# Batch 0's z on the way in: two direct tiles instead of six, group 1's z over four column tiles, a raw load for the state, and a wide state tile of its own for batch 1

## The chip, the cores and the metric

One NeuronCore of a Trainium2 chip runs the kernel. The figure is device time in microseconds of one launch; the kernel before takes 694.18 us in the median of three runs (694.01 to 696.45). TensorE (PE) multiplies, with its weight loads listed apart (PEld); VectorE (DVE), ScalarE (ACT) and GpSimd (POOL) work elementwise; SyncE (SP) issues most DMAs, ACT a few.

## What is computed

Eight batches of 512 tokens and 32 state rows, eight heads of 64. Tokens read the state, the state reads the tokens, and both results, 8 x 544 = 4352 rows of 512, go through a feed-forward layer with a squared ReLU, all in float32:

```python
scores = scale * np.matmul(x, state.transpose(0, 1, 3, 2))        # per batch and head: 512 x 32
a = softmax(scores);   xread = np.matmul(a, state)                # the tokens' result
scores2 = scale * np.matmul(state, x.transpose(0, 1, 3, 2))       # 32 x 512
a2 = softmax(scores2); sread = np.matmul(a2, x)                   # the state's result
y = np.concatenate([xread, sread], axis=2)                        # then as rows (b, s), heads side by side
r = np.maximum(y @ w_in, 0.0)                                     # 512 -> 2048
out = (r * r) @ w_out                                             # 2048 -> 512
```

## The kernel before

**The products.** For the tokens, `xread @ w_in` is not formed from `xread`. Since `xread = a @ state`, the kernel builds `z = state @ w_in` per batch (head by head, 256 rows of (head, state) by 2048 columns), and a unit of work is one batch and one column tile `fc` of 128 columns: an *up* product `ph` = z' a (L773, six matmuls of 512 columns: high by high, low by high, high by low, for two groups of heads), ReLU on ACT (L779), square on DVE or ACT (L785, L787), the split into a high and a low part `g_hi` (ACT) and `g_lo` (DVE, L345), and a *down* product into four accumulators `po` (L809, twelve matmuls). Most operands are such high and low pairs: ACT casts the high part, DVE or POOL subtracts (the helper `split`, L340 and L345).

**The units** run in the order of `PARTS`: batch 0 with column tiles 0 to 5, batch 1 with all sixteen, batch 0 with 6 to 15, then batches 2 to 7, and in the end the state rows of all batches together. The first visit to batch 0 is there while weights still come in; its partial sums go to DRAM and come back.

**z.** Batches 0 to 3 are group 0, 4 to 7 group 1. For group 0, `z_part` (L429) multiplies the state of four batches by two column tiles of `w_in` in plain float32 (L439), 16 blocks in all, two 64-row halves side by side; ACT copies the result to `z_stage` (L464) and stores it to DRAM (`zd`). For group 1 the same function runs in the middle of the kernel with split operands (L451, twelve matmuls of 256 columns a block). `z_fetch` (L500) reads one batch's rows back in four loads of 64 KB and splits them into `z_hi`, `z_lo`. For the first six column tiles (`DIRECT`) of batch 0, `z_direct` (L479) makes z on the spot from a block-diagonal state tile `sp_f` (L486, tile `pzd`), with no way through DRAM.

**Scores.** `sq` (L563) multiplies x by the same `sp_f` for batches 0 and 1; from it come, over transposes `sT` and `pa`, the softmax weights `a_hi`, `a_lo` that an up product needs, and `e2` for the other softmax. Batch 0's state is loaded straight into `sp_f`, batch 1's later copied over it (L535).

**Weights** arrive as 64-bit words and are turned into float32 in four steps each (`singles`, ACT L356, DVE L360, L365, L371): `wi` tiles from `w_in`, `wof` and then `wo_hi`, `wo_lo` from `w_out`. Their raw tiles share four slots (tag `raw`).

**The order** on each engine comes from a planner. Every operation states an engine and a cost, its operands, a due time or earliest time; the planner runs a list schedule for several settings (`FIRST` by `SLACKS`), takes the one that ends first by its own costs, and issues in that order. All engines then run their queues in order, and wait for each other by semaphores. `keep_busy` (L836) gives PE small filler matmuls for planned gaps.

## Time and profile before

| | |
|---|---|
| median of three runs | 694.18 us |
| the profiled execution itself | 694.38 us |
| its span, first to last instruction | 692.6 us |
| PE busy | 682.9 us, 99% |
| ACT, DVE, POOL busy | 432.7, 376.7, 158.7 us |
| granted PE clock | 1.00 throughout |
| first up product (`ph`) starts | 21.40 us |
| batch 1's first up product | 62.79 us |

The profile numbers time from the first instruction. "Busy" of PE counts from the start of a matmul to its modelled end, so that the starts of neighbouring matmuls, not their durations, tell the pace. A row of the timeline gives start, length, engine, source line, what is written from what, how many instructions, and in brackets the idle time before and what ended it.

### The profile page before, as it was taken

The page shows a single profiled execution, that of the slowest core. Times are in us where ns is not written, and L with a number is a line of the kernel's source. Part 1 is how long each engine was busy: PE and PEld are TensorE (multiplying, and loading weights), DVE is VectorE, ACT ScalarE, POOL GpSimd, SP SyncE. Part 2 cuts the span into 40 slices and gives each one's busy share as a digit, 9 for nine tenths or more (in the row PEclk, how much of TensorE's full clock was granted, in tenths as well). Part 3 has the DMA queues.
Part 4 walks back from the last instruction along what each step waited for, and adds up shares of the span by engine and source line. Part 5 has one row for each costly group of instructions (what it writes and reads, how often), then busy time and mean ns, then how long its engine had stood idle before and what let it go on. Part 6 is the DMA issues. An engine that isn't in the chain of part 4 may idle for free.

```text
span 692.6 us, 9920 instructions
## 1 busy us (share of the span) xinstructions
PE 682.9 (99%) x3416; PEld 549.0 (79%) x3416; DVE 376.7 (54%) x657; ACT 432.7 (62%) x819; POOL 158.7 (23%) x174
## 2 busy tenths in 40 slices
PE   8999999999999999999999999999999999999997
PEld 7767777778888887777887888888888888888886
DVE  5999889284386556423342574673853433223431
ACT  4788778686565766666565675775655555443552
POOL 0010003243333354111222353363423210000000
PEclk9999999999999999999999999999999999999999
DMA  8778884352122313533233222222232112100101
GB/s 290 256 268 283 300 289 149 126 185 89 54 91 87 96 46 127 177 141 122 80 117 127 92 78 98 88 91 62 91 102 82 31 31 91 32 1 0 62 1 32
DMA packets 50371, 79.05 MB, mean 114 GB/s; under 512 B 6928, under 2 KB 32656, under 8 KB 50320
## 3 DMA queue, kind: packets, MB, share of 16 engines
q1 hardware_dynamic: 45248, 60.84, 27.4%
q10 hardware_dynamic: 5072, 17.57, 6.4%
q8 instruction: 27, 0.44, 0.3%
q14 instruction: 24, 0.20, 0.1%
HBM read 51.64 MB, written 26.74 MB: 113 GB/s over the span
## 4 chain that ended last, share of the span: by engine, by line
PE 95%; DMA 2%; ACT 1%; DVE 1%; issue 0%; ACTq 0%
PE po L809 55%; PE ph L773 28%; PE pr L714 2%; PE pz L439 2%; PE pz L451 2%; PE pq L584 2%; DMA w_raw<-w_in 1%; PE idle L836 1%; PE pt L696 1%; DMA out<-os__2977 1%; PE sq L563 1%; PE pzd L486 1%; DVE wi L365 0%; ACT z_stage L464 0%; ACT r L779 0%
## 5 line engine op out<-in xcount | busy, mean ns | idle before, releaser
L809 PE MATMUL po<-wo_hi,g_hi 128*128 128x512 f32 x544 | 218.8, 402 | 2.2 <-ACT g_hi L340 1.1
L809 PE MATMUL po<-wo_lo,g_hi 128*128 128x512 f32 x544 | 214.4, 394 | 0.0
L345 DVE TENSOR_TENSOR g_lo<-ph,g_hi 128x512 fp32r<-128x512 f32 (+1 forms) x144 | 94.5, 657 | 138.9 <-PE po L809 108.5
L809 PE MATMUL po<-wo_hi,g_lo 128*128 128x512 f32 x544 | 155.7, 397 | 0.0
L340 ACT CAST g_hi<-ph 128x512 fp32r<-128x512 f32 (+1 forms) x144 | 81.1, 563 | 95.2 <-PE po L809 92.1
L779 ACT ACTIVATE r<-ph 128x512 f32<-128x512 f32 (+1 forms) x144 | 82.7, 574 | 88.9 <-PE ph L773 88.6
L809 PEld LDWEIGHTS po<-wo_hi,g_hi 128*128 128x128 f32 x544 | 102.4, 188 | 28.0 <-ACT g_hi L340 2.0
L809 PEld LDWEIGHTS po<-wo_lo,g_hi 128*128 128x128 f32 x544 | 102.5, 188 | 20.6 <-DVE wo_lo L345 0.2
L809 PEld LDWEIGHTS po<-wo_hi,g_lo 128*128 128x128 f32 x544 | 99.6, 188 | 23.8 <-issue 1.8
L787 DVE TENSOR_TENSOR ph<-ph,r 128x512 f32<-128x512 f32 (+1 forms) x66 | 45.0, 682 | 131.8 <-ACT r L779 131.5
L345 POOL TENSOR_TENSOR xn_hl<-xn_raw,xn_hl 128x512 fp32r<-128x512 f32 x32 | 45.5, 1423 | 193.9 <-ACT xn_hl L340 193.9
L773 PE MATMUL ph<-a_lo,z_hi 128*128 128x512 f32 x256 | 80.9, 396 | 0.0
L773 PE MATMUL ph<-a_hi,z_lo 128*128 128x512 f32 x256 | 80.7, 396 | 0.0
L773 PE MATMUL ph<-a_hi,z_hi 128*128 128x512 f32 x256 | 80.2, 394 | 0.1
L773 PEld LDWEIGHTS ph<-a_lo,z_hi 128*128 128x128 f32 x256 | 48.2, 188 | 11.8
L773 PEld LDWEIGHTS ph<-a_hi,z_lo 128*128 128x128 f32 x256 | 48.1, 188 | 11.1
L773 PEld LDWEIGHTS ph<-a_hi,z_hi 128*128 128x128 f32 x256 | 47.9, 188 | 11.2 <-PE idle L836 0.2
L345 POOL TENSOR_TENSOR xt_hl<-xt_raw,xt_hl 128x512 fp32r<-128x512 f32 x24 | 32.9, 1370 | 81.0 <-ACT xt_hl L340 81.0
L345 DVE TENSOR_TENSOR z_lo<-z_raw,z_hi 128x512 fp32r<-128x512 f32 x61 | 45.3, 742 | 3.0 <-ACT z_hi L340 3.0
L785 ACT ACTIVATE ph<-r 128x512 f32<-128x512 f32 (+1 forms) x78 | 44.4, 569 | 1.9
L464 ACT COPY z_stage<-pz 128x512 f32<-128x512 f32 x64 | 34.5, 592 | 12.1 <-PE pz L451 8.7
L340 ACT CAST z_hi<-z_raw 128x512 fp32r<-128x512 f32 x61 | 37.5, 616 | 2.6 <-DMA z_raw<-zd 2.3
(135 smaller groups left out, 752.6 us busy)
## 6 DMA issues: line engine op xcount, KB each, us to landing
zd<-z_stage ACTq DMA_DIRECT2D x32, 512.0 KB, 3.0
z_raw<-zd SPq DMA_DIRECT2D x244, 64.0 KB, 2.4
w_raw<-w_in SPq DMA_DIRECT2D x16, 512.0 KB, 5.7
wo_raw<-w_out SPq DMA_DIRECT2D x16, 512.0 KB, 5.5
xn_raw<-xn SPq DMA_DIRECT2D x16, 512.0 KB, 4.2
xt_raw<-xT SPq DMA_DIRECT2D x15, 512.0 KB, 3.8
part<-part SPq DMA_DIRECT2D x4, 256.0 KB, 3.5
xt_raw<-xT ACTq DMA_DIRECT2D x1, 512.0 KB, 3.4
```

The lines of the kernel that those rows point to most:

```text
L340: act(n, 0.03 if both else 0.0), lambda e: nc.scalar.copy(out=hi(), in_=src()),
L345: lambda e: ENGINE[e].tensor_sub(out=lo(), in0=src(), in1=hi().bitcast(F32)),
L439: nc.tensor.matmul(pz[i].t[:, q, :], lhsT=st[G].t[own, cc, :], rhs=wi[own, k * FPC:(k + 1) * FPC, cc, :], start=True, stop=True,)
L451: nc.tensor.matmul(pz[i].t[:, q, :], lhsT=s_hl.t[own, m, cc, :], rhs=w_hl[w].t[own, :, cc, :], start=j == 0, stop=j == 2,)
L464: act(512), lambda e, i=i: nc.scalar.copy(out=stage.t[:, :, i, :], in_=pz[i].t),
L584: nc.tensor.matmul(pq.t, lhsT=sp_hl[:, g, q].rearrange("p i n -> p (i n)"), rhs=hl.t[:, i], start=i == 0, stop=i == 1,)
L714: nc.tensor.matmul(pr.t[:, q].rearrange("p i c -> p (i c)"), lhsT=eh.t[:, t, q].rearrange("p i n -> p (i n)"), rhs=hl.t[:, t].rearrange("p ...
L773: nc.tensor.matmul(ph.t[:, :width], lhsT=w, rhs=v, start=j == 0, stop=j == len(pairs_) - 1)
L779: act(width), lambda e: nc.scalar.activation(rl.t[:, :width], ph.t[:, :width], AF.Relu),
L785: nc.scalar.activation(ph.t[:, :width], rl.t[:, :width], AF.Square)
L787: nc.vector.tensor_mul(out=ph.t[:, :width], in0=ph.t[:, :width], in1=rl.t[:, :width])
L809: nc.tensor.matmul(po[t].t, lhsT=(g[0], g[0], g[1])[j].t[:, t * P:(t + 1) * P], rhs=wo[k][j % 2][:, i, :], start=first and j == 0, stop=la ...
```

## The change

Six things change together. `DIRECT` is 2 in place of 6, so batch 0's column tiles 2 to 5 take z from the `z_part` blocks through DRAM. Group 1's blocks are made by a new function `z_quad`: one pair of heads over four column tiles, six matmuls of 512 columns, in place of two pairs over two column tiles, twelve of 256. Batch 0's state comes through a raw tile and two DVE copies, as batch 1's did. Batch 1 has a wide tile of its own, cleared by POOL. `sp_f` is no constant any more but shares a slot with `e_hl`, and its clearing on DVE stands behind that of the filler's operand. And the planner has other costs for matmuls, an earlier `START` and four values of `FIRST`.

```diff
 def pe(n, k=1):
-    return ("PE", k * (0.0134 + n / 2400))
+    return ("PE", k * (0.006 + n / 2265))
...
+    FPQ = 2 * FPC
...
-    DIRECT = 6
+    DIRECT = 2
...
-    START, FIRST, STEP = 14.0, (3.5, 4.4), 4.4
+    START, FIRST, STEP = 8.0, (3.0, 3.5, 4.0, 4.4), 4.4
...
-    sp_f = const.tile([P, NG, 2, P + D], F32, name="sp_f")
-    nc.vector.memset(sp_f, 0.0)
+    sp_f = tile_([P, NG, 2, P + D], F32, "sp_f", "e_hl")
+    op(("DVE", 0.7), lambda e: nc.vector.memset(sp_f.t, 0.0), w=[(sp_f, 0), (sp_f, 1)], due=-90.0)
...
+    def z_quad(kq, g, q, w_hl, begin):
+
+        pz = [tile_([P, FPQ * P], F32, f"pz{i}", "px") for i in range(2)]
+        stage = tile_([P, 2, FPQ * P], F32, "zq_stage", "z_stage")
+        s_hl = halves["st"]
+
+        def products(e):
+            for j, (m, w) in enumerate(((0, 0), (1, 0), (0, 1))):
+                for i in range(2):
+                    own = slice(i * D, (i + 1) * D)
+                    nc.tensor.matmul(
+                        pz[i].t, lhsT=s_hl.t[own, m, g * NQ + q, :], rhs=w_hl[w].t[own, :, q, :],
+                        start=j == 0, stop=j == 2,
+                    )
...
+        src = zq[k // 2][at:at + N, :, :, (k % 2) * FW:(k % 2 + 1) * FW] if b >= GB else zd[k][at:at + N]
...
     def pad(b):
...
-        if b == 0:
-            for i in range(2):
-                load(
-                    lambda i=i: sp_f[rows[i], :, :, at[i]], lambda i=i: src[rows[i]], 32,
-                    w=[f"sp_f{i}"], issue=0.6, due=-60.0,
-                )
-            return
         raw = tile_([P, NG, 2, N], F32, "sp_raw")
-        load(lambda: raw.t, lambda: src, 64, w=[raw])
+        load(lambda: raw.t, lambda: src, 64, w=[raw], due=1e9 if b else -60.0)
         for i in range(2):
             if b < PLAIN_X:
+                if i == 0:
+                    wide[b] = tile_([P, NG, 2, P + D], F32, "sp_f1", "x_hl") if b else sp_f
+                    if b:
+                        op(("POOL", 0.9), lambda e: nc.gpsimd.memset(wide[b].t, 0.0), w=[(wide[b], 0), (wide[b], 1)])
...
-        op(("PE", 0.4), product, w=[ph], begin=0.4 * k)
+        op(("PE", 0.4), product, w=[ph], begin=1.2 + 0.4 * k)
...
-                w_halves(k, At(at - 1))
-                for g in range(NG):
-                    z_part(1, k, g, begin=At(at))
+                w_hl = w_halves(*divmod(m, NG), At(at - 1))
+                for q in range(NQ):
+                    z_quad(*divmod(m, NG), q, w_hl, At(at))
```

**SP, the first loads.** `sp_f` and `sp_raw` are batch state, `w_raw` and `wo_raw` weight tiles, `xt_raw` x for the scores, `st_z` the state for `z_part`. Before:

```order
L379 DMA sp_f<-stP 64x4x32 x2
L379 DMA w_raw<-w_in 128x1024
L379 DMA xt_raw<-xT 128x2x512
L379 DMA w_raw<-w_in 128x1024
L379 DMA wo_raw<-w_out 128x1024
L379 DMA w_raw<-w_in 128x1024
L379 DMA st_z<-stT 64x4x128 x2
L379 DMA sp_raw<-stP 128x128
L379 DMA xt_raw<-xT 128x2x512
```

Now:

```order
L378 DMA sp_raw<-stP 128x128
L378 DMA w_raw<-w_in 128x1024 x3
L378 DMA xt_raw<-xT 128x2x512
L378 DMA st_z<-stT 64x4x128 x2
L378 DMA w_raw<-w_in 128x1024
L378 DMA sp_raw<-stP 128x128
L378 DMA xt_raw<-xT 128x2x512
L378 DMA w_raw<-w_in 128x1024
L378 DMA xt_raw<-xT 128x2x512
L378 DMA w_raw<-w_in 128x1024
L378 DMA wo_raw<-w_out 128x1024 x3
```

Three weight tiles of `w_in` now stand ahead of batch 0's second x tile, and all six that the first visit needs ahead of the first of `w_out`.

**DVE, up to batch 0's second `a_lo`.** Before, the stretch in which both groups' `a_lo` are made:

```order
L643 TENSOR_TENSOR q_270<-q_270,s_313 128x512
L643 TENSOR_TENSOR q_299<-q_299,s_324 128x512
L360 TENSOR_SCALAR wof<-wof 128x512
L360 TENSOR_SCALAR wi<-wi 128x512
L365 SCALAR_TENSOR_TENSOR wof<-wo_raw,wof 128x512
L345 TENSOR_TENSOR a_lo<-pa,a_hi 128x512 x2
L365 SCALAR_TENSOR_TENSOR wi<-w_raw,wi 128x512
L360 TENSOR_SCALAR wi<-wi 128x512 x2
```

Now:

```order
L344 TENSOR_TENSOR a_lo<-pa,a_hi 128x512
L644 TENSOR_SCALAR s_372<-s_372 128x16
L645 RECIPROCAL s_372<-s_372 128x16
L359 TENSOR_SCALAR wi<-wi 128x512
L649 TENSOR_TENSOR q_335<-q_335,s_372 128x512
L364 SCALAR_TENSOR_TENSOR wi<-w_raw,wi 128x512
L359 TENSOR_SCALAR wof<-wof 128x512
L370 SCALAR_TENSOR_TENSOR wi<-w_raw,wi 128x512
L364 SCALAR_TENSOR_TENSOR wof<-wo_raw,wof 128x512
L344 TENSOR_TENSOR a_lo<-pa,a_hi 128x512
L370 SCALAR_TENSOR_TENSOR wof<-wo_raw,wof 128x512
```

The two groups, side by side before, are now one after the other, with steps of weight tiles between; the sixth `w_in` tile is finished ahead of the second `a_lo`.

**PE, from the second up product (before) and the first (now).** Before:

```order
L773 MATMUL ph<-a_hi,z_hi 128x512 x2
L773 MATMUL ph<-a_hi,z_lo 128x512 x2
L773 MATMUL ph<-a_lo,z_hi 128x512 x2
L486 MATMUL pzd<-wi,sp_f 128x128 x8
L809 MATMUL po_467<-wo_hi_85,g_hi 128x512
L809 MATMUL po_467<-wo_lo_86,g_hi 128x512
L809 MATMUL po_473<-wo_hi_85,g_hi 128x512
L809 MATMUL po_473<-wo_lo_86,g_hi 128x512
L486 MATMUL pzd<-wi,sp_f 128x128 x4
```

Now:

```order
L779 MATMUL ph<-a_hi,z_hi 128x512 x2
L779 MATMUL ph<-a_hi,z_lo 128x512 x2
L779 MATMUL ph<-a_lo,z_hi 128x512 x2
L471 MATMUL pz_469<-wi,st_z 128x256
L471 MATMUL pz_470<-wi,st_z 128x256
L471 MATMUL pz_469<-wi,st_z 128x256
L471 MATMUL pz_470<-wi,st_z 128x256
L779 MATMUL ph<-a_hi,z_hi 128x512 x2
L779 MATMUL ph<-a_hi,z_lo 128x512 x2
L779 MATMUL ph<-a_lo,z_hi 128x512 x2
L569 MATMUL sq<-xt_raw,sp_f_119 128x512 x2
```

The direct tiles (`pzd`) are gone from between the up and down products; between the first two up products stands a block of `z_part`, behind them one of batch 1's `sq`.

More of the change, by code (lines that the diff above doesn't have):

```diff
@@ L320, in memory_attention_then_relu2_ffn @@
     ]
-    zd = {
-        (G, k): dr.tile([P, NG, HG, FW], F32, name=f"zd_{G}_{k}")
-        for G in range(NGB) for k in range(NFCH)
-    }
+    zd = [dr.tile([P, NG, HG, FW], F32, name=f"zd_{k}") for k in range(NFCH)]
+    zq = [dr.tile([P, NG, HG, FPQ * P], F32, name=f"zq_{k}") for k in range(NFCH // 2)]
     units = [(b, fc) for b, lo, hi in PARTS for fc in range(lo, hi)]
@@ L418, in z_halves, with w_halves @@
         halves["st"] = hl
-    def w_halves(k, begin):
-        hi, lo = (tile_([P, FPC, NCC, P], F32R, n, "raw") for n in ("wz_hi", "wz_lo"))
-        for i in range(FPC):
+    def w_halves(kq, g, begin):
+        hi, lo = (tile_([P, FPQ, NQ, P], F32R, n, "raw") for n in ("wz_hi", "wz_lo"))
+        for i in range(2):
+            own = slice(i * FPC, (i + 1) * FPC)
             split(
-                lambda i=i: hi.t[:, i], lambda i=i: lo.t[:, i], lambda i=i: wi[:, k * FPC + i], NCC * P,
-                [("wi", k * FPC + i)], [(hi, i)], [(lo, i)], engs=[dve(512), gps(512)], chain="w1", begin=begin,
-            )
-        halves[k] = hi, lo
@@ L430, in z_part, with z_store @@
+    def z_store(pz, stage, out, keys, part, order):
+        for i in range(2):
+            op(
+                act(512), lambda e, i=i: nc.scalar.copy(out=part(i), in_=pz[i].t),
+                r=[pz[i]], w=[(stage, i)],
+            )
+        load(
+            out, lambda: stage.t.rearrange(order), 512,
+            r=[(stage, 0), (stage, 1)], w=keys, eng="ACT", issue=0.35, hold=None, land=4.5,
+        )
+    def z_part(k, g):
         pz = [tile_([P, NQ, FW], F32, f"pz{i}", "px") for i in range(2)]
@@ L506, in z_fetch @@
                 lambda j=j: raw.t[j * N:(j + 1) * N], lambda j=j: src[:, :, j, :], 64,
-                r=[("zd", b // GB, k, g) for g in range(NG)], w=[(raw, j)], issue=0.62, hold=30.0, chain="zf",
+                r=[("zd", b // GB, k, g, q) for g in range(NG) for q in range(NQ)], w=[(raw, j)], issue=0.62, hold=30.0, chain="zf",
             )
@@ L513, in z_fetch @@
         )
-    pairs, kept = {}, {}
+    pairs, kept, wide = {}, {}, {}
     def pad(b):
@@ L563, in product @@
                     nc.tensor.matmul(
-                        sq.t, lhsT=sp_f[:, g].rearrange("p q n -> p (q n)")[:, q * P:(q + 1) * P],
+                        sq.t, lhsT=wide[b].t[:, g].rearrange("p q n -> p (q n)")[:, q * P:(q + 1) * P],
                         rhs=xt.t[:, q, :], start=q == 0, stop=q == NQ - 1,
                     )
-            op(("PE", 1.75), product, r=["sp_f0", "sp_f1", xt], w=[sq])
+            op(("PE", 1.77), product, r=[(wide[b], i) for i in range(2)] + [xt], w=[sq])
             pst = tile_([P, S], F32, "st")
@@ L852, in memory_attention_then_relu2_ffn @@
     for m in range(NFC):
-        z_part(0, *divmod(m, NG))
+        z_part(*divmod(m, NG))
     spill = {}
```

57 lines of the change are left out of this document (21 added, 36 removed).

## The prediction

> **What bounds the kernel now.** I read the page's first lines, then the table by stage, then the waits of TensorE (PE), then the timeline of the first 65 us. Columns of the table: stretch, its length, busy us of PE, PEld, DVE, ACT, POOL with instruction counts, granted clock, DMA share, GB/s.
>
> ```profile
> PE 682.9 (99%) x3416; PEld 549.0 (79%) x3416; DVE 376.7 (54%) x657; ACT 432.7 (62%) x819; POOL 158.7 (23%) x174
> ```
> ```profile
> 0.00:21.40 21.40, 18.97 (x169) 15.12 (x169) 12.69 (x27) 10.96 (x20) 1.17 (x7) 1.00 0.83 284
> ...
> 21.40:62.80 41.40, 40.35 (x207) 30.17 (x206) 40.88 (x80) 33.27 (x68) 3.26 (x2) 1.00 0.76 261
> 62.80:160.00 97.20, 96.01 (x457) 73.05 (x457) 75.39 (x131) 75.14 (x142) 20.34 (x22) 1.00 0.62 213
> ```
> ```profile
> PE idle L836 <- DVE warm L313: 1.8, 1, 1.8
> PE pzd L486 <- DVE wi L371: 1.5, 2, 1.0
> PE po L809 <- ACT g_hi L340: 1.1, 1, 1.1
> PE po L809 <- ACT os__3026 L825: 1.0, 1, 1.0
> ```
>
> PE is full at the full clock, and all its named waits are 5.4 us. So from some 25 us on the time falls only if PE has less to do. Before that PE is not the bound: the first 21.4 us hold much filler, and from 21.4 to 62.8 us DVE is as full as PE (40.88 and 40.35 of 41.40), with ACT at 33.27. Two engines in step is what the change has to deal with; from 62.8 to 160 us DVE has 22 us free.
>
> The rows of the start, then the pace of each engine:
>
> ```profile
> 0.74 0.45 ACTq L379 DMA_DIRECT2D xt_raw<-xT  x1
> 1.69 1.32 SPq L379 DMA_DIRECT2D sp_f<-stP  x2
> 3.06 0.60 SPq L379 DMA_DIRECT2D w_raw<-w_in  x1
> 6.83 0.67 ACT L356 ACTIVATE wi<-w_raw 128x512 f32<-128x512 f32 x1 [4.32 <-DMA w_raw<-w_in]
> 7.53 0.43 DVE L360 TENSOR_SCALAR wi<-wi 128x512 int32<-128x512 int32 x1 [5.79 <-ACT wi L356]
> 8.37 0.83 PE L836 MATMUL idle<-warm 128*128 128x128 bf16 x12
> 9.04 1.94 PE L563 MATMUL sq<-xt_raw,sp_f 128*128 128x512 f32 x4
> 15.69 1.13 PE L439 MATMUL pz<-wi,st_z 64*128 64x256 f32 x8
> 19.12 1.57 PE L439 MATMUL pz<-wi,st_z 64*128 64x256 f32 x8
> 19.93 1.07 ACT L340 CAST a_hi<-pa 128x512 fp32r<-128x512 f32 x2 [0.42 <-ACT z_stage L464]
> 20.55 1.29 DVE L345 TENSOR_TENSOR a_lo<-pa,a_hi 128x512 fp32r<-128x512 f32 x2 [0.79 <-ACT a_hi L340]
> 21.40 0.71 PE L773 MATMUL ph<-a_hi,z_hi 128*128 128x512 f32 x2
> 22.36 0.76 DVE L360 TENSOR_SCALAR wi<-wi 128x512 int32<-128x512 int32 x2
> 25.17 1.89 DVE L371 SCALAR_TENSOR_TENSOR wi<-w_raw,wi 128x512 int32<-128x512 int32 x3
> 26.00 2.02 PE L486 MATMUL pzd<-wi,sp_f 128*128 128x128 f32 x16 [0.99 <-DVE wi L371]
> 34.35 0.45 DVE L535 COPY sp_f<-sp_raw 64x128 f32<-64x128 f32 x2
> 59.62 1.07 ACT L340 CAST a_hi<-pa 128x512 fp32r<-128x512 f32 x2 [0.40 <-PE pa L652]
> 60.58 1.28 DVE L345 TENSOR_TENSOR a_lo<-pa,a_hi 128x512 fp32r<-128x512 f32 x2
> 62.79 2.81 PE ph L773 x12
> ```
>
> Two landmarks: the first up product (`ph`) starts at 21.40 us, and the seventh, batch 1's first, at 62.79. DVE, back to back, takes (1.89 - 0.68) / 2 = 0.60 us for an operation on 512 words and 0.76 - 0.42 = 0.34 for L360. PE takes 0.231 us for a 512-column product:
>
> ```profile
> 291.47 2.05 PE po L809 x8
> 296.75 2.05 PE po L809 x8
> 603.00 2.75 PE po L809 x12
> 607.16 2.75 PE po L809 x12
> ```
> A plain unit is 18 products in 607.16 - 603.00 = 4.16 us; a unit with one of group 1's z blocks in it takes 296.75 - 291.47 = 5.28, so such a block costs 1.12.
>
> **The change part by part.** The sum is made against the profiled execution's own 694.38 us (692.6 of span and 1.8 around it); the median, 694.18, is 0.2 less.
>
> *Four direct z tiles fewer.* Two tiles took 2.02 us in 16 records, so (2.02 - 0.28) / 15 = 0.116 a record and 0.93 a tile of 8: PE loses 3.7 us of work. Its z columns come from the z_part blocks that were run anyway. ACT and DVE trade four half-size splits for two whole ones (0.60 against twice 0.33), nothing. Eight fetches of 64 KB are added; below.
>
> *Quads.* PE's block in the middle of the run, before:
>
> ```profile
> 290.49 0.50 PE L451 MATMUL pz<-wz_hi,st_hl 64*128 64x256 f32 x4
> 290.83 0.28 PE L451 MATMUL pz<-wz_lo,st_hl 64*128 64x256 f32 x2
> 290.95 0.40 PE L451 MATMUL pz<-wz_hi,st_hl 64*128 64x256 f32 x4
> ```
> The two 64-row halves of a pair run together, and a pair of 256 columns takes 290.95 - 290.83 = 0.12 us. Six pairs are 0.72; three pairs of 512 columns, at 0.231 each, 0.69. The rest of the 1.12 lies at the block's two edges, and there are 16 blocks and 32 edges as before. Gain 0.03 x 16 = 0.5 us; bounds 0 and, if the 512-column pair runs at exactly twice 0.107, 1.3. I take 0.4. That goes by what the surplus hangs on: 290.83 - 290.49 is 0.34 for two pairs, the other pairs take 0.12, so it lies where the block begins and ends. The Trainium skill, "TensorEngine Tiling (Array Packing)", section Instruction Overhead, gives each matmul some 60 cycles of overhead; 96 matmuls fewer would then save 2.4 us (an estimate from that page at 2.4 GHz), and the sum would be 2 us lower; the row of 0.12 us for a pair of 256 columns, half of 0.231 and 0.004 more, does not agree.
>
> *The start.* SP's first loads waited for DVE's memset of `sp_f` (1.69) and took 0.66 each, so the first weight tile went out at 3.06. Now one load goes to a raw tile, with no wait; ACT's queue shows that 0.74 is possible, so the weight tile goes out near 1.2, and DVE starts on it 1 to 1.9 us sooner: at 6.0, since it shares the queue with three loads more.
>
> But DVE is given more ahead of the first up. Up to the second `a_lo` of batch 0, before: 16 operations of 0.60, 4 of 0.34, one z_lo of 0.33, four small ones together 0.7: 12.0 us, which from 7.53 to 21.84 took 14.3, so 2.3 us of waits. Now: 24 of 0.60, 7 of 0.34, z_lo, the small ones and four copies into the wide tiles (0.45 a pair): 18.8 us, because all six weight tiles are finished ahead of that `a_lo` instead of two and parts of others. From 6.0, with 1.7 us of waiting for the first `st` copy (the first `sq`, 1.94 us, has to run and be copied): 26.5. DVE is the late engine there, not DMA: six weight tiles, three x tiles and the rest are 5 MB, which the 284 GB/s of the first row move in 18 us. So the **first up starts near 26.3 us instead of 21.4**, 4.9 later. Bounds: 24.8 (no wait) and 27.5 (2.3 us as before and 0.6 for the slower start).
>
> PE meanwhile gets work done that stood behind the first up: one `sq` (1.94) and one z_part (1.13 to 1.57, I take 1.3).
>
> *From first to seventh up.* Before 62.79 - 21.40 = 41.4. Now PE has less between: 3.7 (direct), 1.94 and 1.3 (done earlier), nine `po` of the sixth unit behind the seventh up (9 x 0.231 = 2.1), against four transposes `pt` of 128 columns that came forward (4 x 0.116 = 0.5). 41.4 - 8.5 = 32.9: without waits the seventh up would be at 59.2. DVE's work from `a_lo` of batch 0 to that of batch 1 is 31.4 us by the same count (38.8 before, and there it never waited: 21.84 + 38.8 = 60.6, as the row at 60.58 says), so DVE allows 57.9. ACT's operations between the `a_hi` of batch 0 and of batch 1, each at its mean in the groups, add up to 31 us against 34 before, which took 39.7 (19.93 to 59.62), thus some 5.8 of waits. If ACT waits as long again, batch 1's `a_hi` comes at 25.5 + 36.9 = 62.4 and the seventh up at 63. Between 59.2 and 63, I take 60.9: all three engines now hand to each other with 2 us of slack, and an in-order queue turns such slack into small waits. **1.9 us sooner than before.**
>
> The fetches are covered, though not by much. Column pair 1's second z_part is stored near 21 us and landed at 24. Its fetch stands on SP behind a `wo_raw` load whose slot DVE frees right behind the second `a_lo`, at 27; its four loads leave by 30 and take 5.2, the two splits 1.3: 36.5.
>
> ```profile
> zd<-z_stage ACTq DMA_DIRECT2D x32, 512.0 KB, 3.0
> ```
> ```profile
> z_raw<-zd SPq DMA_DIRECT2D x8, 64.0 KB, 5.2
> ```
> ```profile
> SPq L379 <- DVE wof L371: 22.5, 6, 9.1
> ```
> The first row is the whole run's list of DMA issues, the second that of the first 60 us, the third SP's waits in these 60 us (total, times, longest). PE asks for it at 26.3 plus two ups (2.8), two z_parts (2.6), `sq` (1.94) and twenty `po` (4.6): 38.2. Cover of 1.7 us, and each us past it is a us of PE.
>
> *Behind the seventh up.* PE has the nine `po` to make up, less `pt`: +1.6. The 1.1 us wait for `g_hi` stands where two up products run back to back ahead of a down product; in the new order single ups alternate with downs there: -1.1 (bounds 0 and 1.1). The wait for `os__3026` (1.0) lies where a fourth copy waits for one of three buffers to be written out, and that stays: 0. DVE takes over 44 of the squares that ACT did, and batch 1's wide tile its two copies: with 22 us free up to 160, nothing; were DVE full they would cost 0.60 each.
>
> Sum: -1.9 + 1.6 - 1.1 - 0.4 = -1.8, so 692.6 on the profiled scale and **692.4 us** in the median. Of the 3.7 us taken from PE the slower first up eats about half.
>
> **The rivals.**
> (A) *PE stays dense once it has begun.* Then the seventh up is 1.7 us sooner, and 0.8 more if DVE waits little ahead of the first: -2.5 more, 689.9. For it: in the same stretch before, PE lost 1.05 us in all (40.35 of 41.40); against it: DVE was full there too, and its order is now the one that PE follows.
> (B) *The fetch is late: slower.* Up products 3 to 6 now hang on store, fetch and split. SP's longest wait for a `wof` slot in the first 60 us was 9.1 us. If the fetch of pair 1 stands behind such a wait it goes out at 36 instead of 30 and is split at 42.5: ups 3 and 4 stall for 4 us, and pair 2's, next in the same queue, for 2: 698.4. It decides from 38.2 on. Against it: the slot comes free early in DVE's new order.
> (C) *Cold clock.* The filler ahead of the first `sq` shrinks from 48 matmuls to 32. Before, the filler took 4.97 us:
>
> ```profile
> 1.79 4.97 PE L836 MATMUL idle<-warm 128*128 128x128 bf16 x48 [1.79 <-DVE warm L313]
> ```
> that is 0.10 us apiece, against 0.83 / 12 = 0.07 and less later on, so PE sped up at its end. With 32 the first `sq` could run at half pace, 1.9 us longer, and DVE's chain starts as much later: 694.3. The Trainium skill, "TensorE: Matmul & The Clock Gate", Part 1, says the same of the mechanism: about 3.4 us of activity and not a number of matmuls. The trace agrees in kind: the pace changed 4 to 5 us after the first filler.
> (D) *The quads save more.* If a block's surplus over its columns, 1.12 - 6 x 0.115 = 0.43 us, went with the count of its matmuls and not with its edges, half of it would go, 0.21 x 16 = 3.4, 3.0 more than the sum has: 689.4. The 0.34 of the first two pairs is against it.
>
> **How the numbers follow.** Forecast 0.54 (own range 690.8 to 694.4), A 0.25, B 0.13, C 0.06, D 0.02. A change of under 0.5%, 3.5 us, is about what a measurement here cannot tell from none. Faster than 690.7: A, D and a little of the forecast's edge, less what of A falls short, 0.27. Slower than 697.7: most of B, 0.10. Same: 0.63. The range leaves out A's best (first up at 24.8, `os_` wait gone: 688.2) and B's worse half: 688.8 to 696.2.
>
> **What would show it.** First `ph` between 24.8 and 27.5 us; the seventh between 59.2 and 63; `pzd` with 16 records in place of 48; blocks of `pz` in the middle at 1.09 us instead of 1.12; no PE wait for `z_raw` or its split. I am wrong if the first up starts no later than before, if PE's waits between 26 and 60 us exceed 3 us, or if the stretch behind 160 us differs by over 1.5 us.

## The result: 687.91 us, 6.2 less than before, where 692.4 was predicted

The changed kernel takes 687.91 us (686.67 to 688.96), beside it the kernel before 694.1 (693.56 to 696.45): a ratio of 0.9904, interval 0.9874 to 0.9933. The forecast was 692.4 with a range of 688.8 to 696.2, so the time lies below the range, and the gain is over three times the one I worked out. The span of the one profiled execution fell from 692.6 to 685.5 us, 7.1 us, against 1.8 in the sum.

The table by stage of the changed kernel, cut at the same landmarks: start to the first up product (`ph`), to the seventh (batch 1's first), to the 33rd (batch 2's first), to the end. Columns: stretch, length, then PE, PEld, DVE, ACT, POOL busy with counts, granted clock, DMA share, GB/s.

```profile
0.00:25.69 25.69, 22.18 (x189) 16.56 (x189) 19.55 (x43) 14.16 (x26) 1.85 (x8) 1.00 0.94 336
25.69:58.84 33.15, 31.90 (x163) 23.73 (x161) 32.56 (x63) 28.22 (x59) 2.47 (x2) 1.00 0.73 240
58.84:184.69 125.85, 125.66 (x593) 98.27 (x591) 93.10 (x159) 88.14 (x165) 30.92 (x35) 1.00 0.55 186
184.69:685.50 500.81, 496.31 (x2351) 401.94 (x2349) 272.53 (x454) 267.63 (x511) 123.11 (x131) 1.00 0.24 79
```

The same view of the kernel before, for the two later stretches:

```profile
62.63:188.69 126.06, 124.87 (x591) 96.87 (x590) 87.57 (x151) 91.33 (x171) 29.49 (x35) 1.00 0.53 180
188.69:692.60 503.91, 498.89 (x2455) 407.01 (x2453) 235.74 (x403) 297.28 (x562) 124.82 (x131) 1.00 0.24 78
```

The timeline of the changed kernel at the start and at the two landmarks, and of the kernel before at the seventh up (a closer window puts it at 62.63; the prediction's row, over a longer one, at 62.79):

```profile
0.99 3.60 PE L842 MATMUL idle<-warm 128*128 128x128 bf16 x32 [0.99 <-DVE warm L314]
1.19 1.36 SPq L378 DMA_DIRECT2D w_raw<-w_in  x3
5.11 1.95 PE L569 MATMUL sq<-xt_raw,sp_f 128*128 128x512 f32 x4 [0.52 <-DMA xt_raw<-xT]
6.97 0.43 DVE L359 TENSOR_SCALAR wi<-wi 128x512 int32<-128x512 int32 x1 [2.72 <-ACT wi L355]
25.69 0.71 PE L779 MATMUL ph<-a_hi,z_hi 128*128 128x512 f32 x2
58.84 0.63 PE L779 MATMUL ph<-a_hi,z_hi 128*128 128x512 f32 x2
```
```profile
62.63 0.62 PE L773 MATMUL ph<-a_hi,z_hi 128*128 128x512 f32 x2
```

The four largest waits of PE behind its first filler in the changed kernel (total, times, longest; two more are 0.2 us each):

```profile
PE ph L779 <- DVE g_lo L344: 1.2, 1, 1.2
PE sq L569 <- DMA xt_raw<-xT: 1.0, 2, 0.5
PE pz L471 <- DVE wi L370: 0.7, 1, 0.7
PE pzd L495 <- DVE wi L370: 0.4, 1, 0.4
```

Read against the prediction's fences: the first up is 4.29 us later, the seventh 3.79 sooner, the 33rd 4.00 sooner (184.69 for 188.69), and from there to the end another 3.1 us go, where the sum had 0.4. The waits for `g_hi` at 143 us and for `os__3026` at 277 us are both gone.

The second half can be timed with two rows per kernel, since the order of PE's work hardly differs there: the start of the 65th up (batch 4's first) and of the 121st.

```profile
344.24 0.39 PE L773 MATMUL ph<-a_hi,z_hi 128*128 128x512 f32 x1
601.44 0.39 PE L773 MATMUL ph<-a_hi,z_hi 128*128 128x512 f32 x1
```
```profile
338.48 0.40 PE L779 MATMUL ph<-a_hi,z_hi 128*128 128x512 f32 x1
594.52 0.40 PE L779 MATMUL ph<-a_hi,z_hi 128*128 128x512 f32 x1
```

The first fence is of the kernel before, the second of the changed one: 257.20 and 256.04 us. There is no wait in it and nothing that the change edits but four of the quads' blocks (0.1 us), yet 1.16 us go. PE itself is faster there: from start to start (steps of up to 300 ns between products that follow each other) a product takes 231.9 ns in the mean before and 230.7 now (up products 233.3 and 230.9; the step from an up's first `a_lo` product to its second 238 and 226). So there were three questions: what the start gained and by which part, why the stalls went, and what sets the pace.

### The profile page after: what moved, and what is told of

It reads as the page before. It is cut to its first block, busy times and chain, and to the rows that moved or that the text cites. A ratio compares the mean times of both kernels' runs of the same rounds, so it can differ in the third digit from the quotient of the medians.

```text
span 685.5 us, 9700 instructions
## 1 busy us (share of the span) xinstructions
PE 676.1 (99%) x3288; PEld 540.5 (79%) x3288; DVE 417.7 (61%) x716; ACT 398.1 (58%) x758; POOL 158.4 (23%) x175
## 4 chain that ended last, share of the span: by engine, by line
PE 90%; DVE 6%; DMA 2%; issue 1%; ACT 0%; SPq 0%; DVEq 0%; ACTq 0%
PE po L815 53%; PE ph L779 28%; PE pr L720 2%; PE pz L441 2%; PE pq L590 2%; PE pz L471 2%; PE pt L702 1%; DVE wi L364 1%; DVE wi L370 1%; DVE wi L359 1%; DMA w_raw<-w_in 1%; DMA xt_raw<-xT 1%; DMA z_raw<-zd 1%; DVE wof L364 0%; DVE wof L370 0%
## 5 line engine op out<-in xcount | busy, mean ns | idle before, releaser
L793 DVE TENSOR_TENSOR ph<-ph,r 128x512 f32<-128x512 f32 (+1 forms) x111 | 76.2, 686 | 197.5 <-ACT r L785 197.1
L779 PE MATMUL ph<-a_lo,z_hi 128*128 128x512 f32 x256 | 79.1, 390 | 0.0
L344 DVE TENSOR_TENSOR z_lo<-z_raw,z_hi 128x512 fp32r<-128x512 f32 x63 | 48.6, 772 | 2.0 <-ACT z_hi L339 1.5
L344 POOL TENSOR_TENSOR xt_hl<-xt_raw,xt_hl 128x512 fp32r<-128x512 f32 x24 | 32.9, 1370 | 62.3 <-ACT xt_hl L339 62.3
L649 POOL TENSOR_TENSOR q<-q,s 128x512 f32<-128x512 f32 x13 | 13.7, 1051 | 66.1 <-DVE s L644 45.8
L339 ACT CAST xn_hl<-xn_raw 128x512 fp32r<-128x512 f32 x32 | 19.8, 619 | 12.1 <-PE pr L720 9.4
```

What stands on the lines that cost most here:

```text
L339: act(n, 0.03 if both else 0.0), lambda e: nc.scalar.copy(out=hi(), in_=src()),
L344: lambda e: ENGINE[e].tensor_sub(out=lo(), in0=src(), in1=hi().bitcast(F32)),
L649: two_source(S, b), lambda e: ENGINE[e].tensor_mul(out=q1.t, in0=q1.t, in1=s1.t.broadcast_to([P, NJ, N])),
L779: nc.tensor.matmul(ph.t[:, :width], lhsT=w, rhs=v, start=j == 0, stop=j == len(pairs_) - 1)
L793: nc.vector.tensor_mul(out=ph.t[:, :width], in0=ph.t[:, :width], in1=rl.t[:, :width])
```

## The experiments

All are compared with the kernel before, run beside them. Names: b_ is the kernel before with an edit, a_ the changed kernel with one, n_ the changed kernel without filler in the tail.

| kernel | us | ratio to before | interval |
|---|---|---|---|
| changed kernel | 687.91 | 0.9904 | 0.9874 to 0.9933 |
| b_num | 692.15 | 0.9975 | 0.9958 to 0.9992 |
| b_direct2 | 686.66 | 0.9887 | 0.9864 to 0.9911 |
| b_wide | 691.42 | 0.9956 | 0.9939 to 0.9973 |
| b_quads | 692.84 | 0.9985 | 0.9967 to 1.0004 |
| a_direct6 | 688.66 | 0.9917 | 0.9900 to 0.9935 |
| a_d6_notail | 686.09 | 0.9888 | 0.9871 to 0.9904 |
| b_direct4 | 692.15 | 0.9970 | 0.9958 to 0.9983 |
| a_dveless | 685.88 | 0.9886 | 0.9870 to 0.9903 |
| b_align | 692.94 | 0.9970 | 0.9955 to 0.9984 |
| a_misalign | 691.62 | 0.9962 | 0.9948 to 0.9975 |
| a_notail | 686.66 | 0.9884 | 0.9866 to 0.9901 |
| b_clean | 691.48 | 0.9957 | 0.9943 to 0.9971 |
| n_sb128 | 688.81 | 0.9925 | 0.9904 to 0.9947 |
| n_both128 | 686.70 | 0.9892 | 0.9873 to 0.9911 |
| n_sb192 | 686.43 | 0.9899 | 0.9863 to 0.9935 |
| n_all512 | 680.05 | 0.9796 | 0.9778 to 0.9814 |
| a_place | 681.93 | 0.9825 | 0.9800 to 0.9849 |
| b_place | 686.38 | 0.9888 | 0.9868 to 0.9908 |

### Each part by itself

**b_num: the planner's numbers.**

```diff
-    return ("PE", k * (0.0134 + n / 2400))
+    return ("PE", k * (0.006 + n / 2265))
...
-    START, FIRST, STEP = 14.0, (3.5, 4.4), 4.4
+    START, FIRST, STEP = 8.0, (3.0, 3.5, 4.0, 4.4), 4.4
...
-        op(("PE", 0.4), product, w=[ph], begin=0.4 * k)
+        op(("PE", 0.4), product, w=[ph], begin=1.2 + 0.4 * k)
```

> The kernel before with the planner's numbers of the change alone (cost of a product, START, FIRST, the filler's begin, the two costs of sq and z_part); six direct z tiles, no quads, the old state load. Theory 'order': the 5.3 us by which the change beat my sum come from the order that these numbers set: the stall ahead of the first po behind 143 us (1.4) and the one at 277 us (1.35) are gone here too, the pace of the stretch behind 340 us stays at 4.16 us a unit, and the time is 2.5 to 4 us lower, near 691. Theory 'work': these numbers only fit the plan to less PE work, and with six direct tiles the start is as DVE-bound as before: within 1 us of 694.1, with at least one of the two stalls still there.

1.7 us lower by the ratio, between the two theories. Both stalls are gone, but the new order has others (one of some 0.7 us at 137, 0.5 at 208) and more filler in the tail. A new order trades stalls; it does not by itself bring 5 us.

**b_direct2: two direct tiles.**

```diff
-    DIRECT = 6
+    DIRECT = 2
```

> The kernel before with two direct z tiles in place of six and nothing else. Theory 'work': PE has 3.7 us less to do and the wait for wi at 24.6 us goes too, so 3.5 to 5 us lower, 689 to 690.6. Theory 'order': with the old START and FIRST the first up product is planned as early as before, and DVE's longer way to it turns into PE waits: 1 us lower at most, with named PE waits of over 3 us ahead of 60 us. Both: if the place of the z tiles in memory sets the pace of the up products (here z_hi moves by 12 KB and lies 128 bytes otherwise to a_lo), the a_lo products behind 340 us have another mean than 238 ns; if order sets it, they have it again.

More than either theory has: this one line gains what the whole change does. Its stages:

```profile
0.00:26.16 26.16, 22.70 (x221) 18.42 (x221) 18.37 (x38) 13.73 (x28) 1.16 (x7) 1.00 0.92 319
26.16:59.19 33.03, 32.24 (x155) 23.04 (x153) 32.17 (x64) 27.02 (x52) 2.35 (x2) 1.00 0.78 255
59.19:184.89 125.70, 125.70 (x588) 99.21 (x589) 92.29 (x157) 94.41 (x177) 30.40 (x36) 1.00 0.55 185
184.89:684.70 499.81, 495.25 (x2425) 405.67 (x2423) 233.87 (x399) 296.41 (x562) 124.78 (x131) 1.00 0.24 79
```

The landmarks are those of the full change to half a us, with the old START and the old state load. The other 4 us lie behind 185 us, where this line changes no work: the stall at 277 is gone, the up products run at 231.1 ns, and no filler is left for the tail.

**b_wide: raw state load and a wide tile for batch 1.**

```diff
-                load(
-                    lambda i=i: sp_f[rows[i], :, :, at[i]], lambda i=i: src[rows[i]], 32,
-                    w=[f"sp_f{i}"], issue=0.6, due=-60.0,
-                )
...
+                    wide[b] = tile_([P, NG, 2, P + D], F32, "sp_f1", "x_hl") if b else sp_f
```

> The kernel before with only the raw state load and batch 1's own wide tile. The first weight tile is asked for near 1.2 us in place of 3.06, and DVE starts on it up to 1.5 us sooner. Theory 'DVE bounds the start': the first up comes 1 to 1.5 us sooner and the time is 0.5 to 1.5 us lower, 692.6 to 693.6. Theory 'the start is covered': DVE is back to back from 21 to 63 us anyway, nothing, 694. Both: the constants move by 3 KB here, and all tiles with them; if placement sets the pace of the up products, a plain unit behind 340 us is 4.15 us or less in place of 4.16, another 1 us; if not, 4.16.

3.1 us lower by the ratio, more than either theory. The first up starts at 20.55 us, 0.85 sooner, and the 33rd 2.6 sooner; most of the rest is the missing stall at 277. The up products keep 233.3 ns although the constants moved by 3 KB and the working tiles by other whole KB, so a move by whole KB does not set the pace.

**b_quads: one pair of heads over four column tiles.**

```diff
-                        pz[i].t[:, q, :], lhsT=s_hl.t[own, m, cc, :], rhs=w_hl[w].t[own, :, cc, :],
+                        pz[i].t, lhsT=s_hl.t[own, m, g * NQ + q, :], rhs=w_hl[w].t[own, :, q, :],
```

> The kernel before with only the quads for group 1's z. Theory of the sum: 0.03 us a block, 16 blocks, 0.4 us lower, a unit with a block 5.25 in place of 5.28. Rival D: 0.2 a block, 3.4 us lower, a unit with a block near 5.07. The tiles lie as before, so the a_lo products behind 340 us keep their mean of 238 ns if placement sets it. What else differs is order: the stall at 277 us (1.35) stays if only the new costs remove it.

No difference that can be told from none. A unit with a block takes 5.25 to 5.26 us for 5.28, as the sum had it; rival D is out. The rows are of b_quads, two blocks 5.26 us apart:

```profile
289.34 0.73 PE L441 MATMUL pz<-wz_hi,st_hl 64*128 64x512 f32 x4
294.60 0.73 PE L441 MATMUL pz<-wz_hi,st_hl 64*128 64x512 f32 x4
```

The stall at 277 is gone here as well; that at 143 stays. One by one the ratios add up to 2.0%, 13.7 us; the whole gains 1.0%, 6.2. The parts are substitutes: each takes away some of the same losses.

### Is the saved PE work worth anything?

**a_direct6 and a_d6_notail: the change with six direct tiles**, the second also without the 13 sets of filler in the tail.

```diff
-    DIRECT = 2
+    DIRECT = 6
```
```diff
+            sets[0] += 1
-            for t in range(NT):
+            for t in range(NT if sets[0] <= 27 else 0):
```

> The changed kernel with six direct z tiles in place of two: numbers, quads and the wide tile stay. Theory 'work' (two direct tiles carry the gain): 3.5 to 5 us of the 6.2 go, 691.5 to 693. Theory of additive parts, from the runs of the parts (numbers -1.9, wide -2.7, quads -1.2): 688.3 with six direct tiles too.

> The changed kernel with six direct z tiles and without the 13 sets of filler that stand in the tail. With a_direct6 this says whether the 3.7 us of PE work that two direct tiles save are worth anything beside the rest of the change. Theory 'they are given back': as a_notail, 686.7 plus or minus 0.8. Theory 'work counts': 689 or more.

With the rest of the change in place, the four direct tiles make no difference that can be measured: 688.66 against 687.91, and without tail filler 686.09 against 686.66 (a_notail, below). In the two profiles the last down product starts at 680.39 and 680.38 us. The start of a_direct6:

```profile
0.00:20.26 20.26, 16.63 (x152) 13.10 (x153) 13.82 (x31) 11.13 (x22) 1.85 (x8) 1.00 0.85 289
20.26:57.03 36.77, 36.22 (x192) 26.84 (x190) 35.92 (x72) 28.77 (x58) 3.79 (x3) 1.00 0.82 284
```

DVE is full from the first to the seventh up in both (35.92 of 36.77; 32.56 of 33.15). Two direct tiles save PE 3.4 us of `pzd` up to the seventh up, and up to the 33rd PE runs 32 filler products more (140 for 108), 2.9 us: most of the saved time is waited out, since in that order all six weight tiles pass DVE ahead of the first up.

**b_direct4: half of it, in the kernel before.**

```diff
-    DIRECT = 6
+    DIRECT = 4
```

> The kernel before with four direct z tiles in place of six and nothing else (z_hi lies 128 bytes off, as before). Theory 'work': half of the PE work goes, 1.9 us, beside what the new order does with the three stalls: 690 to 692. Theory 'order': what two direct tiles alone gained (7.4) came from the new order's lack of the stalls at 24.6, 143 and 277 us, from the place of z_hi and from a tail without filler; then four direct tiles gain what their own order sheds of these, whatever the PE work: a unit of 4.16 us (no gain by place), and the difference to the time before is the sum of the stalls and fillers that are gone, within 1 us.

2.1 us lower by the ratio. That agrees with 'work' as well as with 'order' (the last down product starts 3.8 us sooner in the profiles, of which the stalls at 143 and 277 and the fillers are some 3.2; z_hi is 128 bytes off and the up products take 233.3 ns). It tells the two apart too little; a_direct6 does.

**a_dveless: less for DVE ahead of the first up.**

```diff
-            dve(n), lambda e: nc.vector.scalar_tensor_tensor(
+            dve(n), lambda e: less or nc.vector.scalar_tensor_tensor(
                 out=bits(), in0=low(), scalar=29, in1=bits(),
```

> The changed kernel with one DVE operation (0.60 us) left out of each of the first six weight tiles, the one that puts in the bits of the low word; these tiles then lack their last three bits, everything else is computed and ordered as before. 3.6 us of DVE's work ahead of the first up product are gone. Theory 'DVE sets the pace up to the seventh up': the first up comes near 22.5 in place of 25.7, the seventh 3 us sooner, and PE's filler does not move with it; the time is 2 to 3.6 us lower, 684.3 to 686. Rival 'PE sets it' (as in my sum, where PE's products less waits make the stretch): the first up comes sooner but the seventh by less than 1 us, 687 to 688.

The first up starts at 24.19 us, the seventh at 57.94, 0.9 sooner than in the change, and everything behind is 1.2 to 1.4 us sooner; 685.88. So of 3.6 us taken from DVE about a third arrives, if the two profiles are taken as they are: DVE seems to set the pace only until the transfers do. The share is not settled, since the seventh up of the change's own start lies between 58.5 and 61.0 us from profile to profile (below, a_place), and the intervals of the two times overlap. ACT's waits for weight tiles in the first 26 us, of the change and then of a_dveless:

```profile
ACT wi L355 <- DMA w_raw<-w_in: 3.9, 2, 3.8
ACT wof L355 <- DMA wo_raw<-w_out: 0.3, 1, 0.3
```
```profile
ACT wi L355 <- DMA w_raw<-w_in: 4.8, 3, 3.8
ACT wof L355 <- DMA wo_raw<-w_out: 1.4, 2, 0.8
```

The first row of the changed kernel's stages has the DMA engines at 0.94 and 336 GB/s. The start has two bounds close to each other, DVE and the transfers.

### The losses that a new order can shed

**b_align: place alone.** The planner is untouched; two small tiles are claimed ahead of `z_hi`.

```diff
+    plan.ahead.append(lambda: [sb.tile([P, S // 32, 1], F32, name="s1", tag="s1", bufs=2) for _ in range(2)])
...
                 if k.t is None:
+                    if k.tag == "z_hi" and self.ahead:
+                        self.ahead.pop()()
                     k.t = k.make()
```

> The kernel before, every instruction in the same order, but the two small s1 tiles lie ahead of z_hi in memory, so that z_hi moves by 128 bytes and its start is the same modulo 2048 as that of z_lo, a_hi and a_lo (as it is in the changed kernel and with two direct tiles alone; with the numbers, the wide tile or the quads alone it is 128 bytes off, as before). Theory 'place': the second a_lo product takes 224 to 231 ns in place of 240, a plain unit 4.15 us or less in place of 4.16, and over 128 units the time is 1 to 2.2 us lower, 692 to 693. Theory 'order' (the pace comes with the order of the instructions): the pace stays, 238 ns in the mean, and the time is 694.

**a_misalign: the reverse**, an unused gap of 128 bytes behind `z_hi` in the changed kernel.

```diff
+        self.gap = lambda: pool.tile([128, 32], F32, name="gap", tag="gap", bufs=1)
...
                     k.t = k.make()
+                    if k.tag == "z_hi" and not self.gap:
+                        self.gap = k.gap()
```

> The changed kernel, every instruction in the same order, with an unused gap of 128 bytes behind z_hi, so that z_lo, a_hi, a_lo and all behind them lie 128 bytes off z_hi modulo 2048, as before the change. Theory 'place': the second a_lo product goes back from 226 ns to 238, a plain unit from 4.15 to 4.16 us, the time up by 1 to 2 us, 689 to 690. Theory 'order': 687.9 with the pace of the change.

The two rows as above, first of b_align, then of a_misalign:

```profile
344.65 0.40 PE L777 MATMUL ph<-a_hi,z_hi 128*128 128x512 f32 x1
601.13 0.40 PE L777 MATMUL ph<-a_hi,z_hi 128*128 128x512 f32 x1
```
```profile
340.45 0.40 PE L783 MATMUL ph<-a_hi,z_hi 128*128 128x512 f32 x1
598.71 0.40 PE L783 MATMUL ph<-a_hi,z_hi 128*128 128x512 f32 x1
```

256.48 in place of 257.20, and 258.26 in place of 256.04, with the same instructions in the same order. 'Place' holds: up products go from 233.3 to 231.0 ns and from 230.9 to 233.7, and in a_misalign the down products go from 230.7 to 232.7 too, since `g` moved against `wo`. In the whole, 0.3% and, from 0.9904 to 0.9962, 0.6%.

**a_notail: no filler at the end.**

```diff
+            sets[0] += 1
-            for t in range(NT):
+            for t in range(NT if sets[0] <= 35 else 0):
```

> The changed kernel without the last five sets of filler (20 of 160 idle products, all in the last 5 us of PE's work); nothing else moves. Theory 'filler in the way': the sets take 0.8 us and the first po behind each of two of them 0.1 more, nothing waits there, so 1.0 us lower, 686.9. Theory 'filler fills': PE would wait for g_lo in their place, the time is 687.9.

686.66. Two rows of the changed kernel's tail, then of a_notail the 121st up and the last down product:

```profile
676.93 0.40 PE L842 MATMUL idle<-warm 128*128 128x128 bf16 x4
680.38 0.39 PE L815 MATMUL po<-wo_hi,g_lo 128*128 128x512 f32 x1
```
```profile
594.96 0.40 PE L779 MATMUL ph<-a_hi,z_hi 128*128 128x512 f32 x1
679.65 0.39 PE L815 MATMUL po<-wo_hi,g_lo 128*128 128x512 f32 x1
```

From that up to the last product 84.69 us in place of 680.38 - 594.52 = 85.86: 1.2 us, so the filler was in the way and filled nothing.

**b_clean: three losses taken from the kernel before, without any edit of the change** (and `z_hi` placed as in b_align).

```diff
+            copies[0] += 1
-            if e == "ACT":
+            if e == "ACT" and copies[0] != 12:
...
+            for t in range(NT if sets[0] <= 33 else 0):
```

> The kernel before, with none of the change's edits and all instructions in the same order but for three small things: z_hi lies as in b_align, the fourth copy of batch 2's output stands on DVE at its place and not on ACT, and the last seven sets of filler (28 idle products, all in the tail) are left out. Theory 'accidents' (most of the change's gain beyond my forecast is losses of the order before that any new order sheds): 1.2 (place) + 1.35 (the stall at 277 us) + 1.0 (filler in the tail) = 3.5 us lower than before, 690.6, with six direct tiles, no quads and the old state load. Rival 'the change itself': these are small or turn up elsewhere, within 1.2 us of b_align, and the rest of the 6.2 us needs an edit of the change. Known risk: DVE may now wait for the output's write in ACT's place, and PE for DVE.

3.0 us lower by the ratio, the last down product 3.6 sooner (683.97 for 687.56). 'Accidents' holds for about half of the change's gain. Half of the stall at 277 stays, now as a wait of DVE for the same write. How it went in the changed kernel shows in two rows, the fourth copy before and after:

```profile
277.70 0.59 ACT L825 COPY os__3026<-po 128x512 f32<-128x512 f32 x1 [2.58 <-DMA out<-os__2977]
```
```profile
271.36 0.69 DVE L833 COPY os__3010<-po 128x512 f32<-128x512 f32 x1 [0.57 <-DMA out<-os__2961]
```

The first copy's write, for whose buffer the fourth waits, takes 5.8 us to land in the profile of before and 3.6 in that of the change, and the fourth copy has gone to DVE. Neither is an edit. With the order of before the stall was 1.2 us in its own profile, 1.0 in b_place and 0.5 in b_align, and the write took 5.8, 5.6 and 5.0 us, so the stall hangs on how long one write takes. In every kernel with a new order it was gone; in b_num, b_wide, b_quads and b_direct2 the write takes 3.5 to 3.7 us, as in the change, and in b_quads and b_direct2 the fourth copy is still ACT's, so it need not change its engine. What makes the write slow was not settled.

### What of the place decides

The four n_ kernels are a_notail with unused bytes: n_both128 and n_all512 have 128 ahead of the constants (`wo` among them), n_sb128, n_sb192 and n_all512 have 128, 192 and 64 ahead of the working tiles (z, a, g). n_all512, with both:

```diff
+    const.tile([P, 32], F32, name="gap0")
     ident = const.tile([P, P], F32, name="ident")
...
+    sb.tile([P, 16], F32, name="gap", tag="gap", bufs=1)
     with tc.manual_schedule():
```

> a_notail with an unused tile of 128 bytes ahead of all working tiles, so that z, a and g all move by 128 bytes and keep their places to each other, while the constants (wo among them) stay: the working tiles now start at 448 modulo 512 in place of 320. Theory 'relative' (the pace of a product hangs on where its two operands lie to each other): up products (z with a, offset 0 as before) keep 230.9 ns in the mean, down products (g with wo, offset 448 as in a_misalign) go from 230.7 to 232.7, the time up by 3 us, 690. Theory 'absolute' (it hangs on where each operand lies): up products go to 233 or more too, 5 us, 692.

> a_notail with 128 unused bytes ahead of everything, so that constants and working tiles all move by 128 and no two tiles change their places to each other. Theory 'relative': up 230.9 and down 230.7 as in a_notail, the time 686.7. Theory 'absolute': down products change (g at 448 as in a_misalign, 232.7 there), the time 689 or more.

> a_notail with 192 unused bytes ahead of the working tiles, which then start at 0 modulo 512; wo stays at 896. Theory 'absolute': an even start is no worse than 320, up products 230.9 or less, down products 230.7 or less, the time 686.7 or lower. Theory 'relative': up 230.9, and down (g to wo 384 in place of 576) different from 230.7 by 1 ns or more in either direction, 2.4 ns over 1,632 products being 4 us.

> a_notail with constants and working tiles all at 0 modulo 512 (128 unused bytes ahead of the constants, 64 more ahead of the working tiles). Theory 'absolute': as n_sb192 or better. Theory 'relative': up 230.9; down with g to wo at 512 modulo 2048, another pace than in n_sb192. If both paces are lowest here, this is the version to keep, below 686.

The stretch from the 65th to the 121st up is 256.03 us in a_notail. The rows, in the order n_sb128, n_both128, n_sb192, n_all512:

```profile
338.83 0.40 PE L779 MATMUL ph<-a_hi,z_hi 128*128 128x512 f32 x1
596.24 0.39 PE L779 MATMUL ph<-a_hi,z_hi 128*128 128x512 f32 x1
```
```profile
339.55 0.40 PE L780 MATMUL ph<-a_hi,z_hi 128*128 128x512 f32 x1
595.59 0.40 PE L780 MATMUL ph<-a_hi,z_hi 128*128 128x512 f32 x1
```
```profile
339.21 0.39 PE L779 MATMUL ph<-a_hi,z_hi 128*128 128x512 f32 x1
595.44 0.39 PE L779 MATMUL ph<-a_hi,z_hi 128*128 128x512 f32 x1
```
```profile
336.06 0.39 PE L780 MATMUL ph<-a_hi,z_hi 128*128 128x512 f32 x1
589.18 0.39 PE L780 MATMUL ph<-a_hi,z_hi 128*128 128x512 f32 x1
```

257.41, 256.04, 256.23 and 253.12 us; in ns per product, up and down: 229.8 and 233.5, 230.9 and 230.7, 228.7 and 232.5, 226.9 and 228.4. Moving all by 128 bytes changes nothing to a tenth of a ns: 'absolute' falls. Moving the working tiles against `wo` does, 'relative' holds for the down products. It is not the whole rule: the up products, whose own operands kept their places to each other, changed by 1 to 4 ns with the place of `wo`, so a product seems to feel the tiles of its neighbours too; no run isolates that. n_all512, where everything starts at the same place modulo 512, is fastest in both. No run has two of these tiles 256 bytes apart modulo 512, so the step that counts may be smaller than 512.

**a_place and b_place: equal places, in both kernels.** b_place also has the small tiles ahead of `z_hi`, as b_align.

```diff
+    sb.tile([P, 16], F32, name="gap", tag="gap", bufs=1)
     with tc.manual_schedule():
```

> The changed kernel, instructions as they are (filler in the tail too), with one unused tile of 64 bytes ahead of the working tiles: z, a and g then start at 384 modulo 512, and so does wo. Theory 'equal' (PE is fastest when all tiles that it reads start at the same place modulo 512, whatever place): all products at 228 ns as in n_all512, the time down by the same 6 to 7 us that n_all512 was under a_notail, 681 to 682. Theory 'even' (they have to start at a multiple of 512 itself): no better than the change, 686 to 690, with the products at 230 ns or more.

> The kernel before, instructions in the same order, with the same done to it: the small s1 tiles ahead of z_hi as in b_align, and an unused tile of 64 bytes ahead of the working tiles, so that z, a, g and wo all start at 384 modulo 512. Theory 'equal': products from 231.9 ns to 228, over 2,400 products 9 us, 685, which is less than the changed kernel takes as it stands; against a_place it gives what the change's edits are worth when place is the same on both sides: by my ledger 4 us. Theory 'even': as b_align, 693.

First a_place, then b_place:

```profile
338.19 0.39 PE L779 MATMUL ph<-a_hi,z_hi 128*128 128x512 f32 x1
591.32 0.39 PE L779 MATMUL ph<-a_hi,z_hi 128*128 128x512 f32 x1
```
```profile
341.16 0.39 PE L777 MATMUL ph<-a_hi,z_hi 128*128 128x512 f32 x1
593.99 0.39 PE L777 MATMUL ph<-a_hi,z_hi 128*128 128x512 f32 x1
```

253.13 and 252.83 us: 64 bytes are enough, at 384 modulo 512, and 'equal' holds. The kernel before with its tiles so placed takes 686.38, no more than the changed kernel as it stands. Between equal places the change is worth 686.38 - 681.93 = 4.4 us, so of the measured 6.2 some 1.8 were place; both figures have an uncertainty of 2 us or so. n_all512, at 680.05, beats both kernels by 8 and 14 us.

The profile of a_place shows one thing more. Its instructions are those of the changed kernel in the same order, the 32 filler products at the start too, but its first `sq` runs at half the pace: 3.75 us, where the changed kernel's row above has 1.95. The rows of a_place, then DVE's wait for the copy of that `sq`, first in the changed kernel and then in a_place:

```profile
0.99 3.59 PE L842 MATMUL idle<-warm 128*128 128x128 bf16 x32 [0.99 <-DVE warm L314]
5.21 3.75 PE L569 MATMUL sq<-xt_raw,sp_f 128*128 128x512 f32 x4 [0.63 <-DMA xt_raw<-xT]
```
```profile
DVE nm L673 <- ACT st L576: 0.3, 1, 0.3
DVE nm L673 <- ACT st L576: 2.1, 1, 2.1
```

The first up then starts at 27.60 us in place of 25.69 and the seventh at 61.03 in place of 58.84. The profiles of n_sb192 (27.54 and 60.33) and a_d6_notail (21.78 and 59.52, for 20.26 and 57.03 in a_direct6) show the same half pace; the other eight with this filler do not. a_d6_notail and a_direct6 differ only in the tail, so it comes and goes from one execution to the next. Which of the runs without a profile began so is not known. a_place's four times are 680.68, 680.71, 683.15 and 683.28 us, the last being the profiled one; with the lower two alone the change would be worth 5.7 us at equal places, and place 0.5 of the 6.2.

## Why the prediction was wrong

**The start: right to 0.6 us, in part by luck.** First up 25.69 us for 26.3, inside 24.8 to 27.5; the weight tile goes out at 1.19, as said. But DVE began at 6.97 us where I had 6.0, worked 18.2 us up to the second `a_lo` where I had 18.8, and waited 0.4 where I had 1.7: the errors offset each other. `pzd` is 16 records, and PE never waits for `z_raw`, so rival B fails. Rival C fails in this execution: the first `sq` takes 1.95 us as before, after 3.60 us of filler. It is not out for the kernel, since in three of the eleven profiles with this filler the first `sq` did run at half pace, and the first up came 1.5 to 1.9 us later, near the 1.9 that C names. The Trainium skill, "TensorE: Matmul & The Clock Gate", Part 1, with its some 3.4 us of activity, which it says vary from run to run, agrees with both rows: 3.60 us of filler were enough in the changed kernel's profile, and 3.59 us were not in a_place's.

**First to seventh up: the step that failed first.** I had 34.6 us (32.9 of work and 1.7 of waits), and it took 33.15. The 32.9 were never free of waits: the 41.4 of before that I took off from held PE's own wait for `wi` at 24.6 us, 1.15, which the prediction quotes and then counts as work. With that out, PE's work is some 31.7; measured were 33.15 with one wait of 1.25 (`g_lo`), which leaves 31.9. So of the 1.45 us that I had too much, 1.0 is this wait counted as work, and 0.45 the waits that I added on top. Rival A had the seventh up at 58.4 to 59.2 and it came at 58.84, but not for A's reason: PE was no denser than before, idle for 1.25 us of this stretch against 1.05. Nor is one profile exact here. Over the six kernels that share the change's start (the changed kernel, a_notail, a_misalign, n_sb128, n_both128 and n_all512, all with the first `sq` at full pace) the stretch takes 32.8 to 34.0 us, always under 34.6, and the seventh up lies at 58.5 to 60.0.

**The sentence that the slower first up eats half of the 3.7 us** understated it. With six direct tiles in the changed kernel the time is the same as far as these runs can tell, so all of it is eaten. What the start gained, 4 us up to the 33rd up, comes as well from b_direct2's single line as from all the rest without it (a_direct6): the wait at 24.6 and the stall at 143 are shed by either.

**Behind the seventh up.** The `g_hi` wait went, 1.25 us from start to start where I had 1.1. The `os_` wait, costed at 0 with "and that stays", went too: 1.2 us. I had named its mechanism rightly (three buffers, a write on its way) and taken for lasting what hangs on the length of one write, which came out shorter in the new orders named above. The expectations on record put these two at 1.4 and 1.35 and so a little high. Quads: 0.4 in the sum, 5.28 to 5.25 us a unit measured, 0.5. The rule of the Trainium skill, "TensorEngine Tiling (Array Packing)", section Instruction Overhead, taken as 60 cycles on top of each matmul's columns, would have given 2.4; the trace does not bear that reading out here.

**A term was missing.** The change moves `sp_f` out of the constants and alters the order in which working tiles are first claimed, and with that where each lies. I costed it at nothing. It is 1.16 us between 344 and 601 us, and 1.8 in the whole by a_place and b_place, uncertain by 2 us; b_align, which gives the kernel before the changed kernel's places modulo 512, gains 2.1 by the ratio. My own condition, that I am wrong if the stretch behind 160 us differs by over 1.5 us, was met, by these two terms.

Adding up, in us and from one profile of each kernel: the seventh up 1.9 sooner than forecast (0.7 to 2.2 over the six kernels above), the stretch from there to the 33rd up 0.7 shorter (0.15 of it the `g_hi` wait, the rest not traced), the `os_` wait 1.2, the pace 1.2, quads and tail 0.3: 5.3, the difference between 7.1 and 1.8.

What stays open: why the place modulo 512 sets the pace, what makes one output write slow, when the first `sq` runs at half pace, and how the waits of the first 60 us divide between DVE and the transfers.

## What to carry to other kernels

Before costing a change against a trace, take the waits out of the stretch that you cut from, and put a term with two bounds, kept and gone, on each wait that hangs on a coincidence of order: here two of them, `g_hi` and `os_`, were 2.4 of the 7.1 us, though a new order can bring others, as b_num's 0.7 and 0.5. When most of the time is dense PE work, read PE's start-to-start time per product and the addresses of its operands first: 64 unused bytes, added to the changed kernel, were worth 6.0 us, about as much as its six edits. And removed work pays only on the engine that is full at that place; a filler that is planned for the start has to be kept out of the end. And read a landmark of the start from more than one profile: here it moved by over 2 us with the same instructions in the same order.
